# A fused attention and MLP kernel: tiles moved to multiples of 64 bytes, token sums formed a step earlier, five low parts given to GpSimd

## The chip, the cores and the metric

The kernel runs on one core of a Trainium2 chip. The metric is the device time of one execution in microseconds (us). The time before is the median of three runs; the profile is of one further execution.

## The reference

Three layers follow one another on a batch of 4 sequences of 768 tokens, 384 channels:

```
state = f_t * state + k_t v_t^T ;  y_t = q_t state          (gated linear attention, 8 heads of 48, f = sigmoid(f_logit))
u  = x + (U, V mixed over the tokens)                        (rank 32, x = the attention's output)
x2 = u + relu(u @ w_ch1) @ w_ch2                             (384 -> 1536 -> 384)
h  = relu(x2 @ w_in) ; c = conv3(h, conv_w)                  (384 -> 1024, over the tokens)
out = (h * sigmoid(c)) @ w_out                               (1024 -> 384)
```

The weights arrive as 64-bit floats and are turned into 32-bit ones in the kernel.

## The kernel before, in words

**Split products.** A 32-bit operand is held as a high part, rounded to the type F32R that TensorE reads, and a low part, the remainder. One product is then three matmuls: high by high, high by low, low by high. `split(src, hi, lo, eng)` makes the parts: ScalarE copies `src` into `hi` (L113), and the engine `eng` subtracts, `lo = src - hi` (L87).

**Stages.** From 0 to about 157 us the attention and the token mixing run, chunk by chunk. From 157 to 250 us the first MLP runs on the first 1024 tokens (t = 0): for each of its 12 blocks `u` and two halves `i`, `up1` makes 9 matmuls of 512 columns into a PSUM bank `a`, `relu` writes the high part with ScalarE (L287) and the low part with VectorE (L288), and `down1` makes 9 matmuls into the banks `b`. `relu` writes the pair `rh`, `rl`, but every third time one tile named `third` that holds both. During this stage the weights of the next blocks are still being made: three VectorE instructions `cvt` for a piece (L136 to L138), then ScalarE's cast into `w1h` or `w2h` (L113) and GpSimd's subtraction into `w1l` or `w2l` (L87). From 250 to 449 us the same MLP runs on the other two token blocks (t = 1, 2) in six groups each, in a Strassen-like form with sums of weights (`swh`, `swl`) and four sums of token blocks, so that a group has fewer products. From 449 us the second MLP runs with matmuls of 384 columns; they read tokens from `us` or `w2h`, and weights of 384 columns from `w1h`, `w1l`, as the moving operand.

**Two changes of token block.** A group of t reads its tokens from 18 slots of 512 columns: slots 0 to 11 are the tile `us`, slots 12 to 17 the tile `us2`. `value(kk, i, eng)` splits one token block into its slots; `total(n, eng)` makes the sum or difference number n on `eng`, and returns a function that splits it into its slots. Slots 12 and 13 hold the tokens (0, 0), 14 to 17 the sums 1 and 2. Before t = 1 (the first change, 217 to 251 us) these steps hang in the list `after` on steps (u, i) of t = 0. Before t = 2 (the second change, 335 to 355 us) they stand in `group`, and what can't be done in the last group of t = 1 goes into the list `carry`, which the first group of t = 2 empties.

**Order.** Each engine runs its instructions in the order in which the code records them. An instruction that waits holds all behind it on its engine.

**Where tiles lie.** The pools opened with `side="right"` are stacked down from the end of a partition. In the built program `u32` begins at byte 192,480, which is 32 beyond a multiple of 64, and so do `third`, `winh`, `winl`, `swh`, `swl`, `us2` and `spare`, and in the attention stage `uhl`, `vst`, `xh`, `xl`, `zst` and the tiles of queries, keys and values. The tiles `us`, `rh`, `rl`, `w1h`, `w1l`, `w2h`, `w2l` of the left side begin at multiples of 64.

Of the kernel before, what the change touches and what calls it, by code (L numbers as in the profile page):

```python
# [9 lines left out]
F32 = mybir.dt.float32  # L10
# [30 lines left out]
def kernel(  # L41
# [60 lines left out]
    w1l = const.tile([128, KD * DF1], F32R, name="w1l")  # L102
    w2h = const.tile([128, J1, DM], F32R, name="w2h")
    w2l = const.tile([128, J1, DM], F32R, name="w2l")
    u32_p = ctx.enter_context(tc.tile_pool(name="u32_p", bufs=1, side="right"))
    u32 = u32_p.tile([128, KD, B * S], F32, name="u32")
    w1hv = w1h.rearrange("p (a x) -> p a x", a=KD)
# [105 lines left out]
    def mlps(ms, banks, pieces, late, checks, hooks):  # L213
# [7 lines left out]
        u0 = us[:, 0:2 * KD * S].rearrange("p (i k s) -> p i k s", i=2, k=KD)  # L221
# [57 lines left out]
        def relu(ps, u, i):  # L279
            n = len(made)  # L280
            made.append((u, i))
            if win and n % 3 == 2:
                x = third([128, 2 * HT], F32R)
                rh, rl = x[:, 0:HT], x[:, HT:2 * HT]
            else:
                rh, rl = [rg.tile([128, HT], F32R, tag=x, name=x) for x in ("rh", "rl")]
            nc.scalar.activation(out=rh, in_=ps, func=ACTF.Relu)  # L287
            nc.vector.scalar_tensor_tensor(  # L288
                out=rl, in0=ps, scalar=0.0, in1=rh.bitcast(F32), op0=ALU.max, op1=ALU.subtract)
            downs.extend((rh, rl, u, i, m) for m in range(KD))  # L290
# [105 lines left out]
        def turnover(t):  # L396
            x = []
            ve, gp = nc.vector, nc.gpsimd

            def value(kk, i, eng):  # L400
                split(u_block(t, kk, i), *tokens_of(kk, i), eng)

            def total(n, eng):
                if t == 1:
                    dst = spare[0 if n == 3 else 1]
                else:
                    if not x:
                        x.append(ws_p.tile([128, 2 * 384], I32, tag="raw", name="sums", bufs=raw_bufs[0]).bitcast(F32)[:, 0:HT])
                    dst = x[0]
                b11, b12, b21, b22 = [u_block(t, *y) for y in ((0, 0), (0, 1), (1, 0), (1, 1))]  # L410
                a, b = {1: (b12, b11), 2: (b22, dst), 3: (b22, b12), 4: (b21, dst)}[n]
                sub(eng, dst, a, b)
                return lambda eng: split(dst, *token_sum(n), eng)

            return value, total

        n_group, carry = [0], []

        def group(t, p):
            j0, j1 = 2 * p, 2 * p + 1  # L420
            u0, u1 = t * J1 + j0, t * J1 + j1
# [5 lines left out]
            value, total = turnover(t + 1)  # L427
            ve, gp = nc.vector, nc.gpsimd
# [14 lines left out]
            nc.scalar.copy(out=s1, in_=pa)  # L443
            prod(pb, weight_sum(p, 1), token_sum(1), True)
            nc.scalar.copy(out=s5, in_=pb)
            for _ in range(min(2, len(carry))):
                carry.pop(0)()
            later(2)
            down1(2)
# [29 lines left out]
            prod(pw, weights(2, j0), tokens_of(2, 0))  # L479
            relu(pw, u0, 0)  # L480
            if not room:
                total(4, ve)(gp)
            later(room)
            down1(2)
# [1 line left out]
            relu(pz, u1, 1)  # L486
            if not room:
                carry.append(lambda: total(3, ve)(gp))
                carry.append(lambda: value(1, 1, gp))
                carry.extend(lambda a=a: value(*a) for a in ((2, 1, ve), (2, 0, gp), (1, 0, ve)))  # L490
            if ends_all:
                split_u(0)
            down1(1)
# [206 lines left out]
        u0, u1 = J1 - 2, J1 - 1  # L700
        items += [(up1, u0, 0), (up1, u0, 1), (down1, KD), (up1, u1, 0), (down1, KD), (up1, u1, 1), (down1, KD)]
        value, total = turnover(1)
        ve, gp = nc.vector, nc.gpsimd
        t_sums = {}

        def start_sum(n):
            t_sums[n] = total(n, ve)

        def end_sum(n):
            t_sums[n](ve)  # L710

        after = {}
        for p in range(J1 // 2 - 2):
# [2 lines left out]

            for x in range(4):
                after[2 * p + 2 + x // 2, x % 2] = [lambda k=x, f=lazy: f(k)]
        for at, f in (((8, 0), lambda: value(0, 0, ve)), ((9, 0), lambda: start_sum(1)), ((9, 0), lambda: end_sum(1)),
                      ((9, 1), lambda: start_sum(2)), ((9, 1), lambda: end_sum(2)), ((u0, 0), lambda: start_sum(4)),  # L720
                      ((u0, 1), lambda: start_sum(3)), ((u1, 0), lambda: end_sum(3)), ((u1, 0), lambda: value(1, 1, gp)),
                      ((u1, 0), lambda: end_sum(4)), ((u1, 1), lambda: value(1, 0, ve)), ((u1, 1), lambda: value(2, 0, gp)),
                      ((u1, 1), lambda: value(2, 1, ve))):
            after.setdefault(at, []).append(f)
# [32 lines left out]
        for i, (b, j) in enumerate(units):  # L757
# [6 lines left out]
            if i == len(units) - 1:  # L764
                last = gate_end(b, j)
# [23 lines left out]
    gc = gs.enter_context(tc.tile_pool(name="gc", bufs=1, side="right"))  # L789
    wk3 = gs.enter_context(tc.tile_pool(name="wk3", bufs=3, side="right"))  # L790
    wk2 = gs.enter_context(tc.tile_pool(name="wk2", bufs=2, side="right"))
    wk1 = gs.enter_context(tc.tile_pool(name="wk1", bufs=1, side="right"))
# [11 lines left out]
    dr = gs.enter_context(tc.tile_pool(name="gdr", bufs=1, space=bass.MemoryType.DRAM))  # L804
    ends_d = dr.tile([NG, 1, NP * 128], F32, name="ends_d")
    w_t = [gc.tile([MP, NP, D2], F32, name=f"w{i}") for i in range(2)]
    one = gc.tile([128, 1], F32, name="one")
    uhl = gc.tile([128, NCH, 2 * R], F32R, name="uhl")
    vst = gc.tile([3 * R, S], F32R, name="vst")
    a_t = [gc.tile([128, NP, 128], F32, name=f"a{i}") for i in range(3)]  # L810
# [339 lines left out]
    with tc.manual_schedule():  # L1150
# [200 lines left out]
        last = {}  # L1351

        def last_z():
            mix_in(NG - 1)
            last["z"] = mix_z(B - 1)
            last["g"] = g1 = wk1.tile([128, 1], F32, tag="g1", name="g1")
            nc.vector.tensor_reduce(out=g1[0:MP], in_=ga[0:MP].rearrange("p g a -> p (g a)"), axis=mybir.AxisListType.X, op=ALU.min)

        def last_add():
# [185 lines left out]
```

## Time and profile before

| | us |
|---|---|
| median of 3 runs | 653.61 (652.57 to 653.63) |
| profiled execution, whole | 656.3 |
| profiled execution, span of the trace | 654.6 |
| TensorE (PE) busy in the span | 634.9 |
| VectorE (DVE) busy | 456.9 |
| ScalarE (ACT) busy | 305.8 |
| GpSimd (POOL) busy | 192.5 |

The span runs from the first to the last recorded instruction; 1.7 us of the execution lie outside it. The end of a matmul is modelled and neighbours overlap, so that what a stretch of matmuls takes is read from start to start.

### The profile page before, as it was taken

The page shows a single profiled execution, that of the slowest core. Times are in us where ns is not written, and L with a number is a line of the kernel's source. Part 1 is how long each engine was busy: PE and PEld are TensorE (multiplying, and loading weights), DVE is VectorE, ACT ScalarE, POOL GpSimd, SP SyncE. Part 2 cuts the span into 40 slices and gives each one's busy share as a digit, 9 for nine tenths or more (in the row PEclk, how much of TensorE's full clock was granted, in tenths as well). Part 3 has the DMA queues.
Part 4 walks back from the last instruction along what each step waited for, and adds up shares of the span by engine and source line. Part 5 has one row for each costly group of instructions (what it writes and reads, how often), then busy time and mean ns, then how long its engine had stood idle before and what let it go on. Part 6 is the DMA issues. An engine that isn't in the chain of part 4 may idle for free.

```text
span 654.6 us, 12837 instructions
## 1 busy us (share of the span) xinstructions
PE 634.9 (97%) x5098; PEld 552.1 (84%) x5098; DVE 456.9 (70%) x715; ACT 305.8 (47%) x583; POOL 192.5 (29%) x247
## 2 busy tenths in 40 slices
PE   8999989999999989999998999999999999999995
PEld 6778868887887868888886888889999999999995
DVE  5867767786787887555556555668988777777762
ACT  6779757853223234333344333343544644634533
POOL 2167567662666638100033111112120110210000
PEclk9999989999999999999999999999999999999998
DMA  9787798730333310344400122121000200200202
GB/s 179 145 159 141 157 188 153 146 85 2 95 98 97 98 48 26 116 131 127 132 26 25 53 81 80 52 80 41 1 2 1 74 0 1 73 2 1 74 1 77
DMA packets 132953, 50.19 MB, mean 77 GB/s; under 512 B 113316, under 2 KB 128701, under 8 KB 132884
## 3 DMA queue, kind: packets, MB, share of 16 engines
q1 hardware_dynamic: 132884, 49.28, 30.8%
q8 instruction: 42, 0.69, 0.5%
q14 instruction: 27, 0.22, 0.1%
HBM read 44.50 MB, written 4.77 MB: 75 GB/s over the span
## 4 chain that ended last, share of the span: by engine, by line
PE 85%; DMA 4%; DVE 3%; POOL 2%; ACT 1%; issue 1%; SPq 1%; POOLq 0%; ACTq 0%; DVEq 0%
PE b L84 37%; PE a L84 36%; PE y L84 4%; DMA f<-in_f_logit_dram 4%; PE s L84 2%; PE n L84 1%; PE kTp L923 1%; PE qTp L923 1%; PE xt L1066 1%; PE z L84 1%; PE kv L84 1%; PE mix L84 1%; POOL sp L850 1%; POOL qh L889 1%; DVE us L87 1%
## 5 line engine op out<-in xcount | busy, mean ns | idle before, releaser
L84 PE MATMUL a<-us,w1h 128*128 128x512 f32 (+1 forms) x384 | 117.2, 386 | 3.6 <-DVE spare L439 2.4
L84 PEld LDWEIGHTS a<-us,w1h 128*128 128x128 f32 x384 | 71.4, 188 | 18.2 <-DVE spare L439 2.8
L84 PE MATMUL a<-us,w1l 128*128 128x512 f32 (+1 forms) x192 | 74.1, 386 | 0.7 <-POOL w1l L87 0.7
L287 ACT ACTIVATE rh<-a 128x512 fp32r<-128x512 f32 x49 | 29.2, 597 | 92.2 <-PE a L84 88.5
L288 DVE SCALAR_TENSOR_TENSOR rl<-a,rh 128x512 fp32r<-128x512 f32 x49 | 33.8, 690 | 48.8 <-ACT rh L287 48.8
L84 PE MATMUL b<-w1h,swl 128*128 128x384 f32 x192 | 64.5, 336 | 0.0
L84 PE MATMUL b<-w1h,swh 128*128 128x384 f32 x192 | 64.5, 336 | 0.0
L84 PE MATMUL b<-w1l,swh 128*128 128x384 f32 x192 | 64.5, 336 | 0.0
L84 PE MATMUL b<-rh,w2h 128*128 128x512 f32 x147 | 57.4, 390 | 0.0
L84 PE MATMUL b<-rh,w2l 128*128 128x512 f32 x147 | 57.4, 390 | 0.0
L84 PE MATMUL b<-rl,w2h 128*128 128x512 f32 x147 | 57.3, 390 | 0.0
L561 ACT ACTIVATE h<-a 128x384 f32<-128x384 f32 x64 | 30.9, 497 | 33.0 <-PE a L84 25.8
L991 DVE TENSOR_TENSOR p<-s,tri 128x512 f32<-128x512 f32 x48 | 30.9, 686 | 20.0 <-PE s L84 19.8
L84 PEld LDWEIGHTS a<-us,w1l 128*128 128x128 f32 x192 | 36.0, 188 | 9.5 <-POOL w1l L87 2.7
L84 PE MATMUL b<-third,w2h 128*128 128x512 f32 x138 | 43.3, 395 | 0.0
L84 PE MATMUL a<-us,winh 128*128 128x384 f32 x144 | 36.9, 338 | 0.0
L84 PE MATMUL a<-w2h,winh 128*128 128x384 f32 x144 | 36.7, 336 | 0.0
L84 PEld LDWEIGHTS b<-w1l,swh 128*128 128x128 f32 x192 | 36.1, 188 | 0.0
L84 PEld LDWEIGHTS b<-w1h,swl 128*128 128x128 f32 x192 | 36.1, 188 | 0.0
L84 PEld LDWEIGHTS b<-w1h,swh 128*128 128x128 f32 x192 | 36.1, 188 | 0.0
L87 POOL TENSOR_TENSOR w2h<-u,w2h 128x384 fp32r<-128x384 f32 x6 | 10.9, 1815 | 80.0 <-ACT w2h L113 80.0
L84 PEld LDWEIGHTS b<-rh,w2h 128*128 128x128 f32 x147 | 27.6, 188 | 6.1
(200 smaller groups left out, 1506.4 us busy)
## 6 DMA issues: line engine op xcount, KB each, us to landing
raw<-in_moe_w_ch_dram SPq DMA_DIRECT2D x48, 384.0 KB
k<-in_k_dram SPq DMA_DIRECT2D x24, 192.0 KB
q<-in_q_dram SPq DMA_DIRECT2D x24, 192.0 KB
v<-in_v_dram SPq DMA_DIRECT2D x48, 96.0 KB
f<-in_f_logit_dram SPq DMA_DIRECT2D x23, 192.0 KB
raw<-in_moe_w_in_dram SPq DMA_DIRECT2D x8, 384.0 KB
raw<-in_moe_w_out_dram SPq DMA_DIRECT2D x8, 384.0 KB
out_dram<-o SPq DMA_DIRECT2D x8, 192.0 KB
```

The source lines that it names most:

```text
L84: nc.tensor.matmul(out=out, lhsT=lhsT, rhs=rhs, start=start, stop=stop, skip_group_check=True)
L87: eng.tensor_tensor(out=out, in0=a, in1=b, op=ALU.subtract)
L287: nc.scalar.activation(out=rh, in_=ps, func=ACTF.Relu)
L288: nc.vector.scalar_tensor_tensor(out=rl, in0=ps, scalar=0.0, in1=rh.bitcast(F32), op0=ALU.max, op1=ALU.subtract)
L561: nc.scalar.activation(out=h[:, 1 + hf.start:1 + hf.stop], in_=ps, func=ACTF.Relu)
L850: nc.gpsimd.tensor_scalar(out=sp, in0=ft.pop(g), scalar1=LARGEST, scalar2=LEAST_LOGIT, op0=ALU.min, op1=ALU.max)
L889: (nc.gpsimd if g == 1 else eng).tensor_tensor(out=heads(q_t[g % 2]), in0=qt.pop(g), in1=heads(a_t[g % 3]), op=ALU.mult)
L923: nc.tensor.transpose(out=ps[:, p, :], in_=src[:, p, 0:MP], identity=ident)
L991: nc.vector.tensor_tensor(out=t, in0=sc[g][j], in1=tri.unsqueeze(1).to_broadcast([128, NP, C]), op=ALU.mult)
L1066: nc.tensor.transpose(out=ps[:, m * 128:(m + 1) * 128], in_=u32[:, m, g * C:(g + 1) * C], identity=ident)
```

## The change

A tile of 32 bytes, `edge`, is put at the very end of each partition, ahead of `u32`, and two one-column tiles take 64 bytes in place of 32. All the tiles named above then begin at multiples of 64 bytes (`u32` at 192,448); no instruction of the computation changes its shape by it. At the first change of token block the sums are formed a step ahead of their casts. At the second change `value(1, 1)` moves out of `carry` into the last group of t = 1, the first step of the next group takes one item of `carry` in place of two, and the low parts of (2, 1) and (1, 0) go from VectorE to GpSimd.

```diff
+    edge = ctx.enter_context(tc.tile_pool(name="edge", bufs=1, side="right"))
+    edge.tile([128, 8], F32, name="edge")
     u32_p = ctx.enter_context(tc.tile_pool(name="u32_p", bufs=1, side="right"))
...
-            for _ in range(min(2, len(carry))):
+            if carry:
                 carry.pop(0)()
...
             if not room:
+                value(1, 1, gp)
                 total(4, ve)(gp)
...
                 carry.append(lambda: total(3, ve)(gp))
-                carry.append(lambda: value(1, 1, gp))
-                carry.extend(lambda a=a: value(*a) for a in ((2, 1, ve), (2, 0, gp), (1, 0, ve)))
+                carry.extend(lambda a=a: value(*a, gp) for a in ((2, 1), (2, 0), (1, 0)))
...
-        for at, f in (((8, 0), lambda: value(0, 0, ve)), ((9, 0), lambda: start_sum(1)), ((9, 0), lambda: end_sum(1)),
-                      ((9, 1), lambda: start_sum(2)), ((9, 1), lambda: end_sum(2)), ((u0, 0), lambda: start_sum(4)),
+        for at, f in (((8, 0), lambda: value(0, 0, ve)), ((8, 1), lambda: start_sum(1)), ((9, 0), lambda: end_sum(1)),
+                      ((9, 1), lambda: start_sum(2)), ((u0, 0), lambda: end_sum(2)), ((u0, 1), lambda: start_sum(4)),
                       ((u0, 1), lambda: start_sum(3)), ((u1, 0), lambda: end_sum(3)), ((u1, 0), lambda: value(1, 1, gp)),
...
-    one = gc.tile([128, 1], F32, name="one")
+    one = gc.tile([128, 16], F32, name="one")[:, 0:1]
...
-            last["g"] = g1 = wk1.tile([128, 1], F32, tag="g1", name="g1")
+            last["g"] = g1 = wk1.tile([128, 16], F32, tag="g1", name="g1")[:, 0:1]
```

VectorE at the first change, from the ReLU's low part of (9, 0) to that of (10, 0), before. `spare<-u` is the subtraction that forms a sum, `us_3123<-spare` (the tile `us2`) its low part:

```order
L288 SCALAR_TENSOR_TENSOR rl<-a_3607,rh 128x512
L136 TENSOR_SCALAR cvt<-raw 128x384
L137 SCALAR_TENSOR_TENSOR cvt<-raw,cvt 128x384
L138 SCALAR_TENSOR_TENSOR cvt<-raw,cvt 128x384
L87 TENSOR_TENSOR spare<-u_76 128x512
L87 TENSOR_TENSOR us_3123<-spare,us_3123 128x512
L288 SCALAR_TENSOR_TENSOR rl<-a_3643,rh 128x512
L136 TENSOR_SCALAR cvt<-raw 128x384
L137 SCALAR_TENSOR_TENSOR cvt<-raw,cvt 128x384
L138 SCALAR_TENSOR_TENSOR cvt<-raw,cvt 128x384
L87 TENSOR_TENSOR spare<-u_76,spare 128x512
L87 TENSOR_TENSOR us_3123<-spare,us_3123 128x512
```

The same place of the changed program (lines are 2 higher there):

```order
L87 TENSOR_TENSOR spare<-u_80 128x512
L290 SCALAR_TENSOR_TENSOR rl<-a_3612,rh 128x512
L138 TENSOR_SCALAR cvt<-raw 128x384
L139 SCALAR_TENSOR_TENSOR cvt<-raw,cvt 128x384
L140 SCALAR_TENSOR_TENSOR cvt<-raw,cvt 128x384
L87 TENSOR_TENSOR us_3127<-spare,us_3127 128x512
L290 SCALAR_TENSOR_TENSOR rl<-a_3647,rh 128x512
L138 TENSOR_SCALAR cvt<-raw 128x384
L139 SCALAR_TENSOR_TENSOR cvt<-raw,cvt 128x384
L140 SCALAR_TENSOR_TENSOR cvt<-raw,cvt 128x384
L87 TENSOR_TENSOR spare<-u_80,spare 128x512
L290 SCALAR_TENSOR_TENSOR third<-a_3681,third 128x512
```

The first sum now stands ahead of the ReLU's low part of (9, 0), and its own low part after the next conversions; the second sum's low part has moved behind the conversions that follow `third`.

VectorE at the second change, in the first group of t = 2, before. `u_76<-b` is the last addition of `down1`, L439 the two additions of the Strassen form, `us<-u_76` the low parts of (2, 1) and (1, 0):

```order
L325 TENSOR_TENSOR u_76<-b_3922,u_76 128x512
L439 TENSOR_TENSOR a_4505<-a_4504,spare 128x512
L87 TENSOR_TENSOR us<-u_76,us 128x512 x2
L325 TENSOR_TENSOR u_76<-b_3926,u_76 128x512
L325 TENSOR_TENSOR u_76<-b_3880,u_76 128x512
L439 TENSOR_TENSOR spare<-a_4504,spare 128x512
L288 SCALAR_TENSOR_TENSOR rl<-a_4505,rh 128x512
```

The changed program at this place:

```order
L327 TENSOR_TENSOR u_80<-b_3926,u_80 128x512
L441 TENSOR_TENSOR a_4511<-a_4510,spare 128x512
L327 TENSOR_TENSOR u_80<-b_3930,u_80 128x512
L327 TENSOR_TENSOR u_80<-b_3884,u_80 128x512
L441 TENSOR_TENSOR spare<-a_4510,spare 128x512
L290 SCALAR_TENSOR_TENSOR rl<-a_4511,rh 128x512
```

The two low parts are gone from between the two additions.

GpSimd over the last group of t = 1 and the first of t = 2, before (`us_3123` is `us2`; `sums` holds a sum of token blocks):

```order
L87 TENSOR_TENSOR us_3123<-u_76,us_3123 128x512
L87 TENSOR_TENSOR us_3123<-sums,us_3123 128x512 x2
L87 TENSOR_TENSOR us<-sums,us 128x512 x2
L87 TENSOR_TENSOR us<-u_76,us 128x512 x2
L87 TENSOR_TENSOR w1l<-cvg,w1h 128x3x128 x8
```

The changed program:

```order
L87 TENSOR_TENSOR us_3127<-u_80,us_3127 128x512
L87 TENSOR_TENSOR us_3127<-sums,us_3127 128x512 x2
L87 TENSOR_TENSOR us<-u_80,us 128x512
L87 TENSOR_TENSOR us<-sums,us 128x512 x2
L87 TENSOR_TENSOR us<-u_80,us 128x512 x3
L87 TENSOR_TENSOR w1l<-cvg,w1h 128x3x128 x8
```

The low part of (1, 1) stands between the sums 2 and 4, and three low parts follow sum 3 where two did. The rows of PE and SP are the same in both programs but for lines and numbers.

## Rows read from the trace of the kernel before

**Rows 1.** Windows: stretch, its us, PE, PEld, DVE, ACT, POOL busy, clock, DMA.

```profile
157.00:226.00 69.00, 68.97 (x302) 55.89 (x301) 54.37 (x71) 17.44 (x34) 39.71 (x51) 1.00 0.29 87
226.00:242.00 16.00, 14.08 (x59) 10.32 (x58) 13.82 (x20) 5.07 (x10) 7.32 (x9) 1.00 0.23 74
344.00:355.00 11.00, 8.63 (x38) 6.68 (x36) 8.97 (x11) 4.83 (x9) 5.01 (x4) 1.00 0.11 36
449.00:655.00 206.00, 197.86 (x1138) 196.93 (x1136) 153.96 (x185) 97.49 (x172) 15.62 (x9) 0.99 0.07 24
```

**Rows 2.** Timeline, PE: start, us, instruction; a block of third, one of rh and rl.

```profile
213.30 0.63 PE L84 MATMUL b<-third,w2h 128*128 128x512 f32 x2
...
215.40 0.63 PE L84 MATMUL a<-us,w1h 128*128 128x512 f32 x2
...
217.49 0.39 PE L84 MATMUL b<-rh,w2h 128*128 128x512 f32 x1
...
219.53 0.62 PE L84 MATMUL a<-us,w1h 128*128 128x512 f32 x2
```

**Rows 3.** Groups of instructions by line, whole span: count, busy, mean ns.

```profile
L84 PE MATMUL b<-third,w2h 128*128 128x512 f32 x138 | 43.3, 395 | 0.0
```

**Rows 4.** Timeline, PE, products of tokens (0, 0) and sum 1 in a group of t = 1.

```profile
296.91 0.63 PE L84 MATMUL a<-us,w1h 128*128 128x512 f32 x2
...
298.31 0.40 PE L84 MATMUL b<-rh,w2h 128*128 128x512 f32 x1
```

**Rows 5.** Timeline, PE, two halts at the first change, in brackets idle time and releaser.

```profile
231.67 0.39 PE L84 MATMUL b<-rh,w2l 128*128 128x512 f32 x1
232.50 0.73 PE L84 MATMUL a<-us,w1h 128*128 128x512 f32 x2 [0.45 <-ACT w1h L113]
...
233.92 0.62 PE L84 MATMUL a<-us,w1h 128*128 128x512 f32 x2
...
239.15 0.39 PE L84 MATMUL b<-rh,w2l 128*128 128x512 f32 x1
240.32 0.73 PE L84 MATMUL a<-us,w1h 128*128 128x512 f32 x2 [0.78 <-ACT w1h L113]
...
241.74 0.63 PE L84 MATMUL a<-us,w1h 128*128 128x512 f32 x2
```

**Rows 6.** Timeline, DVE, the same place.

```profile
226.56 0.69 DVE L288 SCALAR_TENSOR_TENSOR rl<-a,rh 128x512 fp32r<-128x512 f32 x1 [0.96 <-ACT rh L287]
...
229.05 1.25 DVE L138 SCALAR_TENSOR_TENSOR cvt<-raw,cvt 128x384 int32<-128x384 int32 x1
...
231.59 0.69 DVE L87 TENSOR_TENSOR us<-spare,us 128x512 fp32r<-128x512 f32 x1 [0.69 <-ACT us L113]
...
239.17 0.56 DVE L138 SCALAR_TENSOR_TENSOR cvt<-raw,cvt 128x384 int32<-128x384 int32 x1
```

**Rows 7.** Timeline, ACT, the same place.

```profile
230.94 0.62 ACT L113 CAST us<-spare 128x512 fp32r<-128x512 f32 x1 [4.00 <-DVE spare L87]
...
231.95 0.50 ACT L113 CAST w1h<-cvt 128x384 fp32r<-128x384 f32 x1
```

**Rows 8.** Timeline, POOL, the same place.

```profile
240.35 1.00 POOL L87 TENSOR_TENSOR w1l<-cvt,w1h 128x384 fp32r<-128x384 f32 x1 [2.03 <-ACT w1h L113]
```

**Rows 9.** Timeline, POOL, DVE and PE at the second change.

```profile
348.57 3.00 POOL L87 TENSOR_TENSOR us<-u,us 128x512 fp32r<-128x512 f32 x2
...
348.83 3.29 DVE L87 TENSOR_TENSOR us<-u,us 128x512 fp32r<-128x512 f32 x2
...
350.06 0.62 PE L84 MATMUL a<-us,w1h 128*128 128x512 f32 x2
...
351.21 0.39 PE L84 MATMUL a<-us,w1l 128*128 128x512 f32 x1
...
353.24 0.67 DVE L439 TENSOR_TENSOR spare<-a,spare 128x512 f32<-128x512 f32 x1
...
353.97 0.73 PE L84 MATMUL a<-us,w1h 128*128 128x512 f32 x2 [2.37 <-DVE spare L439]
```

## The prediction

> **What bounds the kernel now.** I read the busy time by stretch first. From 157 us to the end TensorE is the pace: it is busy for 68.97 of 69.00 us up to 226, and for 197.86 of the last 206, where what is missing is the tail behind the last matmul [rows 1]. It halts in two places only, both at a change of token block: 226 to 242 us has 1.92 us without a matmul, 344 to 355 us has 2.37 [rows 1]. So time can come from two sources: the step from one matmul to the next, and these two halts. The attention stage ahead of 157 us is a mixture of waits on transfers, GpSimd, VectorE and TensorE; nothing in the change takes work off it.
>
> **Part 1, the addresses.** The reader should compare two blocks of nine matmuls with 512 columns that read the same weights. With `third` as moving operand, 32 bytes beyond a multiple of 64, the nine start at 213.30 and the next block at 215.40: 2.10 us, 233.3 ns each. With `rh` and `rl`, at multiples of 64, it is 217.49 to 219.53: 2.04 us, 226.7 ns each [rows 2]. The difference is 6.6 ns, some 16 of the 512 columns at 2.4 GHz, as if one more piece of 64 bytes were fetched; the reason doesn't matter for the sum.
>
> How many pay it: `third,w2h` has 138 records [rows 3], and the third matmul of each product reads `third` with `w2l`, so 207 in all, and 207 x 6.6 ns = 1.37 us. In the groups of t = 1 and 2 the product of tokens (0, 0) and that of sum 1 have their moving operand in `us2`. Those six take 296.91 to 298.31, 1.40 us, again 233.3 ns each [rows 4]. Sum 2 lies in `us2` too, and the product of sum 3 reads its weights from `swh`, `swl`: six more matmuls for which I have no block as clean; their excess is put between 0 and 6.6 ns, and I take the middle, 3.3. Per group that is 6 x 6.6 + 6 x 3.3 = 59 ns, in 12 groups 0.71 us. Part 1 gives 2.1 us.
>
> In the last stage nothing comes from it: all moving operands (`us`, `w2h`, `w1h`, `w1l`) lie at multiples of 64 already. In the attention stage the products of `xh`, `xl` and `vst` move too (about 72 matmuls, 0.5 us at 6.6 ns), but there others end the waits: I take 0 and keep 0.5 as a bound. So part 1 lies between 0 (if the 6.6 ns have another cause) and 2.6 us.
>
> The Trainium skill (SBUF — State Buffer, Specifications) speaks against this part: it gives SBUF cachelines of 16 bytes and a penalty for crossing into a new one. An offset of 32 is a whole number of such lines, so by that page the shift would change nothing. The trace doesn't agree, since the two blocks differ by 6.6 ns a matmul [rows 2]; what the page would make of the sum is rival B.
>
> **Part 2, the first change.** Two halts. From the start at 231.67 to that at 233.92 there are four matmuls, 0.91 us at 226.7 ns, but 2.25 us passed: 1.34 lost. From 239.15 to 241.74 it is 2.59, so 1.68 lost [rows 5]. (The idle times in brackets are shorter, since the restart itself is slow.)
>
> The first halt waits for `w1h`. Its conversion on VectorE ends at 229.05 + 1.25 = 230.30 [rows 6], but ScalarE casts it at 231.95 only. What stands between: ScalarE is held for 4.00 us by the cast of sum 1, which waits for VectorE's `spare`, and the ReLU and the cast of `w1h` stand behind it [rows 7]. In the changed order sum 1 is formed ahead of the ReLU's low part of (9, 0), where VectorE waited 0.96 us anyway [rows 6], so its 0.6 us is hidden there. (Without that cover it would delay the low part by 0.6 us, which a later block of `down1` reads.) ScalarE's cast of the sum then runs at once, the ReLU of (9, 1) when its product ends, and the cast of `w1h` at about 230.6. With 0.5 for it [rows 7] and 1.00 for GpSimd's `w1l` [rows 8] both are there by 232.1. TensorE wants `w1h` at 231.67 + 0.23 = 231.90 and `w1l` two matmuls later, at 232.35. The first halt goes: 1.34 us.
>
> The second halt waits for the next `w1h`, whose conversion ends at 239.17 + 0.56 = 239.73 [rows 6]. VectorE went from 230.30 to 239.73 without a pause but two: it formed two sums, each followed by a wait of 0.69 us for ScalarE's cast ([rows 6] show one; the other is its like) and a low part. The step of such a 0.69 us instruction to the next is about 0.6. The change takes out of this stretch sum 1 (0.6), both waits (1.4) and sum 2's low part (0.6), together 2.6. It puts in a wait for the ReLU of (10, 0), which VectorE now reaches too early, about 0.6. So the conversion ends 2.0 us earlier, at 237.7, the cast at 238.2, `w1l` at 239.3. TensorE comes 1.34 us earlier as well: it wants `w1h` at 239.38 - 1.34 = 238.04 and `w1l` at 238.5. A halt of about 0.8 us remains, and 0.8 of the 1.68 is won (bounds 0 and 1.68). What is late next is again `w1l`. Sums 4 and 3 stand together later, 1.2 us ahead of the ReLU's low part of (11, 0). Before they stood one step apart, and VectorE is idle there soon after; I put it at 0. Part 2 gives 1.34 + 0.8 = 2.1 us, bounds 1.3 and 3.0.
>
> **Part 3, the second change.** TensorE starts its last matmul before the halt at 351.21 and the next at 353.97 [rows 9]: 2.76 us for 0.23, 2.5 lost. It waits for VectorE's addition `spare` (L439), which frees its bank. Ahead of it on VectorE stand the two low parts, 3.29 us, and two additions of 353.24 - (348.83 + 3.29) = 1.1 us [rows 9]. Without the low parts the additions are done about 350.0. The addition `spare` itself needs the product before 350.06, whose last results land about 0.2 us later. It runs from about 350.3 to 350.95, and TensorE comes at 351.44. The halt goes: 2.5 us.
>
> The cover is GpSimd. It starts its low parts behind sum 3 at 348.57 and took 1.5 us for each [rows 9]. At that price (2, 1) is ready at 350.1, (2, 0) at 351.6, (1, 0) at 353.1. By the code's order TensorE takes (1, 1) at 350.06, (2, 1) three matmuls later, its low part one after that: 350.98, then (2, 0)'s at about 352.4 and (1, 0) behind nine more matmuls, near 354.9. Each is in time, by 0.8 us or more. (1, 1) itself moved ahead of sum 4: one more cast on ScalarE (0.6) and one more low part on GpSimd (1.5), while the slots of (1, 1) have been read. Sum 3 has to wait until GpSimd has read sum 4, so up to 1.5 us could be passed on to it. In the bounds I let part 3 fall to 1.0. The shorter first pop of `carry` changes only which step records what; the low parts are behind sum 3 either way. DMAs aren't moved.
>
> **Sum.** 2.1 + 2.1 + 2.5 = 6.7 us. The profiled execution, 656.3 us, would be 649.6. It is 2.7 above the median of the runs, and that is in no row that the change touches, so I take the 6.7 off the median: 653.6 - 6.7 = **646.9 us**.
>
> **Rivals.**
> - B: the 6.6 ns are not of the address (both halves of `third` are in one tile, `rh` and `rl` in two), or come from a source that stays. For: the nine matmuls from 215.40 to 217.49, between the two blocks compared, read `us` at multiples of 64 and took 2.09 us all the same [rows 2]; something else makes some blocks slow as well. Against: `us2` has no such pair and pays the same [rows 4]. Without part 1: 649.0. By the skill's page named above this is the case to expect.
> - C: VectorE remains the pace at the first change. Per half step it has a ReLU part, three conversions and one or two sums, some 4.4 us against 4.1 of TensorE's 18 matmuls. Then the first halt's gain is met again at the second and 3 is all that goes: 653.6 - 2.1 - 2.5 = 649.0.
> - D: GpSimd's queue takes the place of VectorE at the second change. It decides from 350.98 - 348.57 = 2.4 us for a low part on; the row has 1.5. Then most of part 3 is lost: 649.4.
> - E, the other side: with every tile at the same offset, reads of TensorE fall together with writes of ScalarE and VectorE that lay apart before, and each product pays. There are some 1,280 matmuls from 157 to 449 us (292 us at about 0.228) and 1,138 recorded behind that [rows 1]; against 4.6 us from parts 2 and 3 it costs time from 2.5 ns a product ((4.6 + 1.3) / 2,420). At 6.6 ns it is 16 us: 653.6 - 4.6 + 16 = 665. Against: `rh` and `rl` are written and read at multiples of 64 and are the fast ones [rows 2].
>
> **Chances.** My forecast, all three parts within their bounds: 0.60, with 645 to 648.5 as its own range. B 0.15, C 0.10, D 0.08, E 0.03, and 0.04 that several gains fail and under 1.3 us is left. A measurement of this kernel tells about 0.2% (1.3 us) from no change; the three runs span 1.1. Faster by more: 0.93, within: 0.04, slower: 0.03. The range takes the low bounds (part 1 at 2.6, part 2 at 3.0, part 3 at 2.5: 645.5, and half a microsecond of spread) and, above, cases B to D with the same spread: 645.0 to 650.0.
>
> **What would show it.** Right: `third` blocks at 2.04 us; in 226 to 242 us one halt in place of two, of about 0.8 us; none in 344 to 355; ScalarE's `us<-spare` with no wait for VectorE. Wrong: `third` still at 2.10 (B); a halt at `w1h` ended by VectorE of over 1.5 us (C); a halt behind 350 us ended by GpSimd's `us` (D); matmuls of the last stage further apart than now (E). A longer attention stage would upset the sum without touching any of its terms.

## The result, and the profile after

| | before | after |
|---|---|---|
| median of 4 runs each, us | 653.62 (652.57 to 654.92) | 646.67 (644.27 to 647.38) |
| ratio | | 0.9886 [0.9854, 0.9919] |
| profiled execution, whole | 656.3 | 646.12 |
| span of the trace | 654.6 | 644.4 |

The changed kernel is 6.95 us faster by the medians. The two profiled executions differ by 10.2 us, more than the medians do; where the other 3 us lie is told below.

Windows of the changed kernel by stretches of [rows 1] (the place of the old halt, 353.97 us before, is now at 346.03, so the stretch ahead of it is added). Columns: stretch, its us, busy time of PE, PEld, DVE, ACT, POOL with the number of instructions, granted clock, DMA share, GB/s.

```profile
226.00:242.00 16.00, 15.54 (x67) 12.13 (x66) 14.95 (x22) 6.20 (x12) 7.55 (x8) 1.00 0.17 49
...
250.00:344.00 94.00, 93.44 (x413) 77.06 (x412) 51.02 (x88) 34.80 (x62) 20.83 (x26) 1.00 0.31 97
344.00:355.00 11.00, 11.00 (x50) 9.13 (x49) 6.08 (x11) 3.51 (x6) 3.06 (x3) 1.00 0.11 36
```

At the first change TensorE is without a matmul for 0.46 us where it was 1.92 [rows 1]; in 344 to 355 us nothing is missing where 2.37 were. In their place stands a gap of 0.56 us in 250 to 344. The same stretch of the kernel before has none:

```profile
250.00:344.00 94.00, 94.00 (x410) 76.78 (x410) 50.38 (x88) 32.20 (x57) 21.31 (x30) 1.00 0.32 97
```

Timeline of TensorE in the changed kernel: start, us, instruction, in brackets idle time and releaser.

```profile
210.69 0.61 PE L84 MATMUL b<-third,w2h 128*128 128x512 f32 x2
...
212.73 0.61 PE L84 MATMUL a<-us,w1h 128*128 128x512 f32 x2
...
214.82 0.39 PE L84 MATMUL b<-rh,w2h 128*128 128x512 f32 x1
...
235.08 0.39 PE L84 MATMUL b<-rh,w2l 128*128 128x512 f32 x1
235.59 0.73 PE L84 MATMUL a<-us,w1h 128*128 128x512 f32 x2
236.67 0.50 PE L84 MATMUL a<-us,w1l 128*128 128x512 f32 x1 [0.35 <-POOL w1l L87]
237.01 0.63 PE L84 MATMUL a<-us,w1h 128*128 128x512 f32 x2
...
296.88 0.62 PE L84 MATMUL a<-us,w1h 128*128 128x512 f32 x2
...
298.24 0.62 PE L84 MATMUL a<-us,w1h 128*128 128x512 f32 x2
...
338.82 0.39 PE L84 MATMUL a<-us,w1l 128*128 128x512 f32 x1
339.76 0.72 PE L84 MATMUL a<-us,swh 128*128 128x512 f32 x2 [0.56 <-DVE third L290]
340.33 0.40 PE L84 MATMUL a<-us,swl 128*128 128x512 f32 x1
```

Three things are to be seen. The nine matmuls with `third` go from 210.69 to 212.73, 2.04 us where [rows 2] had 2.10, and six with the tokens (0, 0) and sum 1 from 296.88 to 298.24, 1.36 where [rows 4] had 1.40: all at 226.7 ns. The `us` block behind `third` still takes 2.09. The two halts of [rows 5] have become one: from 235.08 to 237.01 there are four matmuls, 0.91 us at 226.7 ns, but 1.93 us passed, so 1.0 is lost, and the last to come is GpSimd's `w1l`. And there is a new halt at 339.76: from 338.82 to 340.33 there are three matmuls, 0.68 us, and 1.51 passed: 0.83 lost.

What the engines beside it do there, timelines of VectorE, ScalarE and GpSimd in the changed kernel:

```profile
222.86 0.95 DVE L87 TENSOR_TENSOR spare<-u 128x512 f32<-128x512 f32 x1
...
227.58 0.68 DVE L87 TENSOR_TENSOR us<-spare,us 128x512 fp32r<-128x512 f32 x1
...
234.43 0.56 DVE L140 SCALAR_TENSOR_TENSOR cvt<-raw,cvt 128x384 int32<-128x384 int32 x1
...
336.07 1.76 DVE L87 TENSOR_TENSOR sums<-u,sums 128x512 f32<-128x512 f32 x1 [0.19 <-POOL us L87]
339.01 0.69 DVE L290 SCALAR_TENSOR_TENSOR third<-a,third 128x512 fp32r<-128x512 f32 x1 [1.18 <-ACT third L289]
```

```profile
224.18 0.62 ACT L115 CAST us<-spare 128x512 fp32r<-128x512 f32 x1
...
235.02 0.51 ACT L115 CAST w1h<-cvt 128x384 fp32r<-128x384 f32 x1 [0.89 <-DVE cvt L140]
...
337.87 0.62 ACT L115 CAST us<-sums 128x512 fp32r<-128x512 f32 x1 [2.20 <-DVE sums L87]
338.39 0.59 ACT L289 ACTIVATE third<-a 128x512 fp32r<-128x512 f32 x1
```

```profile
235.61 1.01 POOL L87 TENSOR_TENSOR w1l<-cvt,w1h 128x384 fp32r<-128x384 f32 x1 [2.03 <-ACT w1h L115]
...
336.00 1.29 POOL L87 TENSOR_TENSOR us<-u,us 128x512 fp32r<-128x512 f32 x1
...
343.26 3.79 POOL L87 TENSOR_TENSOR us<-u,us 128x512 fp32r<-128x512 f32 x3
```

At the first change, sum 1 is formed at 222.86 and cast at 224.18 without a wait; the 4.00 us for which it held ScalarE [rows 7] are gone, and so is VectorE's 0.69 ahead of the low part [rows 6]. What is left is a chain for the second `w1h`: conversion until 234.43 + 0.56 = 234.99, cast at 235.02, `w1l` from 235.61 to 236.62, matmul at 236.67.

At the second change read the chain backwards from 339.76: TensorE waits for VectorE's low part of `third` (339.01), that for ScalarE's ReLU (338.39), that stands on ScalarE behind the cast of sum 4 (337.87), and the cast waited 2.20 us for the sum, which took 1.76 us on VectorE. Beside it GpSimd runs the low part that the change moved here, `value(1, 1)`, from 336.00 to 337.29. Alone the same subtraction takes 0.69 us (as in the experiment `e4_early_value`, below). The sum ends at 337.83, 0.54 after GpSimd, so it seems hardly to have moved while GpSimd ran. The order itself makes the two meet: sum 4 is written over sum 2, so VectorE has to wait for GpSimd's low part of sum 2 (the 0.19 us in its row), and as that ends GpSimd goes on with (1, 1). ScalarE's extra cast isn't what is late, since ScalarE is idle for 2.20 us behind it. The slow sum agrees with the Trainium skill (SBUF — State Buffer, section SBUF: two separate sides), which says that a VectorE instruction with two inputs from SBUF and a GpSimd instruction that reads SBUF hold one pair of ports in turn, each for the whole instruction.

Of the low parts, those of (2, 1) and (1, 0) are the two that are new to GpSimd; the title's five is not what the program shows.

**The sum.** To leave the attention stage aside I measure from one fixed matmul (the 1,500th of the program, near 148 us before and 146 after) to the start of the last: 498.45 us before, 491.56 after, 6.9 less. That is as much as the medians differ. It consists of the first change, halts of 3.02 and now 1.0 (2.0 us); of the second, 2.64 with the slow restart and now 0.83 (1.8); and of 3.0 for shorter steps, counted as what the steps between consecutive recorded matmuls take over 226.7 ns (512 columns) in the first MLP: 0.96 + 2.59 us before (t = 0; t = 1 and 2), 0.52 + 0.01 after.

**The other 3 us of the profiled executions.** Of these 2.3 lie ahead of the fixed matmul and 1.0 behind the start of the last one. Windows of the kernel before, and then of the changed one, in the attention stage:

```profile
93.00:97.00 4.00, 3.62 (x53) 2.68 (x55) 2.87 (x5) 3.15 (x8) 3.81 (x6) 0.62 1.09 211
94.00:97.00 3.00, 2.72 (x43) 2.15 (x47) 2.22 (x5) 2.96 (x8) 2.81 (x5) 0.50 1.07 205
```

```profile
93.00:97.00 4.00, 3.85 (x99) 3.46 (x101) 3.34 (x7) 3.96 (x10) 3.73 (x6) 1.00 0.90 195
```

In the profiled execution of before TensorE stood at a granted clock of 0.50, which is 1.2 GHz, from 94 to 97 us, and recorded 53 matmuls in 93 to 97 us where the changed kernel has 99. This doesn't follow the change: `e1_addresses` (below), with the change's addresses, has 0.57 over 93 to 97 us, and `e2_first_change` and `e3_second_change`, without them, have 1.00. It fits that the profiled execution of before lay 2.7 us over its median. What the 1.0 us behind the last matmul is, the runs don't tell.

### The profile page after: what moved, and what is told of

Read it like the earlier page. It is cut to its first block, busy times and chain, and to the rows that moved or that the text cites. A ratio compares the mean times of both kernels' runs of the same rounds, so it can differ in the third digit from the quotient of the medians.

```text
span 644.4 us, 12837 instructions
## 1 busy us (share of the span) xinstructions
PE 630.6 (98%) x5098; PEld 551.7 (86%) x5098; DVE 455.5 (71%) x713; ACT 305.8 (47%) x583; POOL 195.4 (30%) x249
## 5 line engine op out<-in xcount | busy, mean ns | idle before, releaser
L87 POOL TENSOR_TENSOR us<-u,us 128x512 fp32r<-128x512 f32 (+1 forms) x16 | 21.7, 1368 | 41.3 <-ACT us L115 41.2
```

What stands on the lines that cost most here:

```text
L87: eng.tensor_tensor(out=out, in0=a, in1=b, op=ALU.subtract)
```

## The experiments

The first three make one part of the change alone in the kernel before, the fourth moves one step in the changed kernel; they ran with the kernel before on one chip (median 654.73 of 24 runs). The others ask what in the addresses counts; the kernel before took 654.05 us beside those with names in `e5` to `e8` and 655.71 beside those in `f` (medians of 7).

### The addresses alone

```diff
+    edge = ctx.enter_context(tc.tile_pool(name="edge", bufs=1, side="right"))
+    edge.tile([128, 8], F32, name="edge")
...
-    one = gc.tile([128, 1], F32, name="one")
+    one = gc.tile([128, 16], F32, name="one")[:, 0:1]
```

and the same for `g1`.

> The kernel before with the address part alone (edge and the two 64-byte tiles), both orders as before. Theory: the step of 226.7 ns holds everywhere behind 250 us, and the time from the first matmul of the first MLP to the last falls by the 3.2 us that the steps above 226.7 ns sum to in the trace before (3.5 us there, 0.3 in the changed kernel): about 650.5. Rival (the address does nothing of its own, the steps shortened because the halts went): the blocks of third stay at 2.10 us, 653.6.

Measured: 652.46 us, ratio 0.9964 [0.9941, 0.9987]. The steps alone give all of part 1: outside the two changes the stretches are as in the changed kernel, 3.0 us shorter than before. The two halts of the first change stay (1.5 and 1.7 us), and so does the one at 350 us. But the profiled execution shows a price behind that halt. Windows and timeline of this kernel:

```profile
350.00:356.00 6.00, 4.42 (x13) 3.50 (x14) 3.48 (x7) 1.78 (x3) 0.00 (x0) 0.75 0.00 0
```

```profile
348.69 0.39 PE L84 MATMUL a<-us,w1l 128*128 128x512 f32 x1
351.58 0.74 PE L84 MATMUL a<-us,w1h 128*128 128x512 f32 x2 [2.50 <-DVE spare L441]
...
354.04 0.63 PE L84 MATMUL b<-third,w2l 128*128 128x512 f32 x1
...
355.32 0.63 PE L84 MATMUL b<-third,w2l 128*128 128x512 f32 x1
```

Behind a wait of 2.50 us the granted clock fell (0.75 over these 6 us), and three matmuls from 354.04 to 355.32 take 1.28 us, 427 ns each in place of 227. Over the 60 matmuls about this change it cost 1.5 us (18.03 against 16.50). So this run shows part 1 at 3.0 less 1.5 (496.92 us from the fixed matmul to the last, 1.5 less than before), and a halt can cost more than its own length. The other runs fit: of the 12, the five with a mean granted clock of 0.996 or more took 649.31 to 650.66 us, near the 650.5 expected, and the seven with 0.993 to 0.995 took 652.38 to 655.58.

### The order at the first change alone

```diff
-        ... ((8, 0), lambda: value(0, 0, ve)), ((9, 0), lambda: start_sum(1)), ((9, 0), lambda: end_sum(1)),
-            ((9, 1), lambda: start_sum(2)), ((9, 1), lambda: end_sum(2)), ((u0, 0), lambda: start_sum(4)),
+        ... ((8, 0), lambda: value(0, 0, ve)), ((8, 1), lambda: start_sum(1)), ((9, 0), lambda: end_sum(1)),
+            ((9, 1), lambda: start_sum(2)), ((u0, 0), lambda: end_sum(2)), ((u0, 1), lambda: start_sum(4)),
```

> The kernel before with the first change of token block alone. Theory: from the start of the matmuls of (9, 0) to those of (11, 0) 2.0 us fall away, one halt of about 1.0 us is left there; blocks of third stay at 2.10 us and the halt of 2.5 us near 351 us stays: about 651.6. Rival (VectorE is the pace, the gain comes only together with the shorter steps): both halts keep 2.5 us or more, 653.6.

Measured: 653.22 us, ratio 0.9972 [0.9959, 0.9985]. Windows and timeline of TensorE in this kernel:

```profile
226.00:242.00 16.00, 15.54 (x67) 12.05 (x66) 14.92 (x22) 5.77 (x12) 7.40 (x10) 1.00 0.20 62
...
350.00:356.00 6.00, 5.60 (x17) 4.45 (x18) 2.94 (x5) 1.78 (x3) 0.00 (x0) 0.72 0.00 0
```

```profile
236.29 0.39 PE L84 MATMUL b<-rh,w2l 128*128 128x512 f32 x1
...
237.87 0.50 PE L84 MATMUL a<-us,w1l 128*128 128x512 f32 x1 [0.35 <-POOL w1l L87]
238.21 0.63 PE L84 MATMUL a<-us,w1h 128*128 128x512 f32 x2
```

The same one halt remains (236.29 to 238.21: 1.92 for four matmuls, 1.0 lost), so part 2 gives its 2.0 us without the others. The 60 matmuls about this change take 14.76 us in place of 16.75. Here too the clock fell behind the halt at 350 us (0.72), which hides 1.5 us of it in this profile.

### The order at the second change alone

```diff
-            for _ in range(min(2, len(carry))):
+            if carry:
                 carry.pop(0)()
...
+                value(1, 1, gp)
                 total(4, ve)(gp)
...
-                carry.append(lambda: value(1, 1, gp))
-                carry.extend(lambda a=a: value(*a) for a in ((2, 1, ve), (2, 0, gp), (1, 0, ve)))
+                carry.extend(lambda a=a: value(*a, gp) for a in ((2, 1), (2, 0), (1, 0)))
```

> The kernel before with the second change alone. Theory: the halt of 2.6 us near 351 us goes, and a new one of about 0.8 us stands some 12 us earlier, where VectorE's subtraction for sum 4 takes 1.8 us instead of 0.7 beside GpSimd's low part of (1, 1): net 1.8, about 651.8. Rival (the halt of 0.8 us comes from the shorter steps, not from the order): no new halt, 651.1.

Measured: 652.17 us, ratio 0.9968 [0.9953, 0.9983]. One row tells what it gives: the matmuls with `swl`, 36 of them, of which the first and the last are the same two products in every kernel here. From the first start to the last it is the groups of t = 1 and 2 with the second change between. The view is the tile `swl` on TensorE: count, duration in ns (least, median, most), first and last start. The kernel before, and this one:

```profile
L84 PE MATMUL a<-us,swl x36: 389/393/401, 250.5 to 431.7; 128*128 128x512 f32 x36
```

```profile
L84 PE MATMUL a<-us,swl x36: 389/393/401, 247.7 to 426.9; 128*128 128x512 f32 x36
```

181.2 us before, 179.2 here: 2.0 us, where 1.8 was expected. The new halt is there with the old, longer steps as well, 1.36 us for three matmuls, 0.68 lost. Timeline of TensorE in this kernel:

```profile
342.14 0.40 PE L84 MATMUL a<-us,w1l 128*128 128x512 f32 x1
342.94 0.73 PE L84 MATMUL a<-us,swh 128*128 128x512 f32 x2 [0.41 <-DVE third L288]
343.50 0.39 PE L84 MATMUL a<-us,swl 128*128 128x512 f32 x1
```

So the order makes it, not the faster steps.

### The low part of (1, 1) a step earlier

In the changed kernel, `value(1, 1, gp)` goes from ahead of `total(4)` to right behind the ReLU before it, where GpSimd's low part ends before VectorE wants to form sum 4.

```diff
             relu(pb, u0, 1)
+            if not room:
+                value(1, 1, gp)
             prod(pa, weights(1, j1), token_sum(4))
...
             if not room:
-                value(1, 1, gp)
                 total(4, ve)(gp)
```

> The changed kernel with value(1, 1) not ahead of sum 4 but two products earlier, behind the ReLU of its first bank. Theory: GpSimd is then done with (1, 1) before VectorE forms sum 2, sum 4 takes 0.7 us again, and the halt of 0.8 us at the second change goes: about 645.9. Rival (ScalarE's extra cast, not GpSimd's low part, is what held the ReLU of third): the cast is as long at its new place and a halt of 0.5 us or more stays, 646.7.

Measured: 646.05 us (642.82 to 646.66), ratio 0.9852 [0.983, 0.9874] to the kernel before. Timelines of VectorE and TensorE, and the row of `swl`, of this kernel:

```profile
336.67 0.69 DVE L87 TENSOR_TENSOR sums<-u,sums 128x512 f32<-128x512 f32 x1 [0.18 <-POOL us L87]
```

```profile
339.42 0.39 PE L84 MATMUL a<-us,w1l 128*128 128x512 f32 x1
339.64 0.62 PE L84 MATMUL a<-us,swh 128*128 128x512 f32 x2
```

```profile
L84 PE MATMUL a<-us,swl x36: 389/389/389, 246.3 to 422.4; 128*128 128x512 f32 x36
```

Sum 4 takes 0.69 us again, the halt is gone, and the stretch is 176.1 us; in the changed kernel it is 176.9 (below). Taking the overlap away takes the halt away, which shows its mechanism. This kernel has the lowest median of the study, but only the trace shows the 0.8 us: the medians (646.05, and 646.67 for the changed kernel, taken at another time) can't tell the two apart.

### Everything at 32 beyond a multiple of 64

Is it the multiple of 64? Without `edge` the right side begins at 32 mod 64 again, and 32 bytes ahead of `w1h` move the left side there too.

```diff
+    const.tile([128, 8], F32, name="pad")
     w1h = const.tile([128, KD * DF1], F32R, name="w1h")
...
-    edge = ctx.enter_context(tc.tile_pool(name="edge", bufs=1, side="right"))
-    edge.tile([128, 8], F32, name="edge")
```

> The changed kernel without the edge and with 32 bytes put ahead of w1h on the left side: every tile that the products of 384 and 512 columns read begins 32 beyond a multiple of 64, moving operands and weights alike. Theory A (a moving operand that begins 32 beyond needs one more piece of 64 bytes): all products of 512 columns step at about 233 ns, 1,250 x 6.6 ns = 8 us slower than the changed kernel, and those of 384 columns behind 449 us also step 5 ns or more later (1,150 x 5 = 6 us): 655 to 661. Theory B (what costs is that moving operand and weights lie differently): all steps at 226.7 and 173.3 ns, 646.7, though nothing lies at a multiple of 64.

Measured: 649.67 us, ratio 0.9935 [0.9913, 0.9957]. The row of `swl` in the changed kernel, then in this one:

```profile
L84 PE MATMUL a<-us,swl x36: 389/389/397, 245.7 to 422.6; 128*128 128x512 f32 x36
```

```profile
L84 PE MATMUL a<-us,swl x36: 389/389/398, 248.3 to 425.2; 128*128 128x512 f32 x36
```

176.9 us in both. With no operand at a multiple of 64 every step is as short as in the changed kernel, and from the fixed matmul to the last it is 491.40 us (491.56 there). So a multiple of 64 isn't what counts in these stages; what the two kernels have in common is that both sides begin at the same place. The total missed both forecasts, 649.67 where theory B had 646.7: the attention stage took 2.5 us longer in this profile, with more waits of TensorE for ScalarE and GpSimd, and all four runs (649.00 to 650.15) are slower than the changed kernel's. Its tiles moved too; whether their place costs something there, these runs don't tell.

### Third, or the weights, out of step

Three kernels move one group of tiles in the changed one. To make room, three small tiles were joined, and that moved the whole left side by 64 bytes as well, which wasn't meant; the places that came about are in the table below.

```diff
-                x = third([128, 2 * HT], F32R)
+                x = third([128, 2 * HT + 16], F32R)[:, 8:2 * HT + 8]
```

(`e7_third_at_16` has 4 in place of 8, for 16 bytes.)

```diff
             mw = ms.enter_context(tc.tile_pool(name="mw", bufs=1, side="right"))
+            mw.tile([128, 8], F32, name="pad0")
             win.extend(mw.tile([128, KD, 128 * W_IN], F32R, name=n) for n in ("winh", "winl"))
             sw.extend(mw.tile([128, (J1 // 2) * 3 * 128], F32R, name=n) for n in ("swh", "swl"))
+            mw.tile([128, 8], F32, name="pad1")
```

> The changed kernel with third alone begun 32 beyond a multiple of 64. Both theories: blocks of nine with third at 2.10 us, 207 x 6.6 ns = 1.4 us. Open: whether neighbouring blocks with other operands get slower too, as those at 2.07 to 2.09 us in the trace before; if so 1.4 to 2.4 us between the first and the last product of 512 columns, if not 1.4.

> The changed kernel with third alone begun 16 beyond a multiple of 64. If any offset from 64 brings one more piece (theory A), or operands that lie differently (theory B): 2.10 us a block as at 32. If the loss grows with the bytes beyond 64 it is less, about 2.07; if pieces of 16 or 32 bytes are what counts, 2.04 at 16 only in the first case.

> The changed kernel with winh, winl, swh and swl alone begun 32 beyond a multiple of 64; they are only ever weights. Theory A (only the moving operand counts): all steps as in the changed kernel. Theory B (operands that lie differently): the products of the three sums, 108 matmuls of 512 columns, step at 232 ns or more, about 0.6 us over both token blocks, and the stage behind 449 us stays at 173.3 ns as it did before.

Measured, one run each: 651.95, 652.72 and 647.9 us. The steps with `third` as moving operand take 233 ns at 32 bytes and 231.8 at 16; those with `swh`, `swl` as weights 32 bytes off take 231.9 in the third kernel. So either operand counts. By the Trainium skill's cacheline of 16 bytes alone (SBUF — State Buffer, Specifications) all three would be without effect, 16 and 32 being whole lines; the runs don't agree, with 5 to 7 ns a matmul. But in the first two also the last stage, where `third` isn't read, was slower, and the shift of 64 is the only other thing that differs there. That led to the next four.

### The left side moved by 64, 128 and 256 bytes

In the changed kernel a row buffer of 512 bytes moves into the last stage's tiles, and the room goes into a pad ahead of `w1h`. All tiles stay at multiples of 64.

```diff
-    low_row = const.tile([1, 128], F32, name="low_row")
+    rows = {}
...
+    const.tile([128, 16], F32, name="pad")
     w1h = const.tile([128, KD * DF1], F32R, name="w1h")
```

(32 and 64 columns for 128 and 256 bytes. A fourth has no pad, but `third` 32 bytes on, as above, in a tile that is 512 bytes longer, so that nothing else moves.)

> The changed kernel with the tiles of the left side (us, rh, rl, w1h, w1l, w2h, w2l and the weight pieces) moved by 64 bytes, net of 512 bytes taken out below them by moving one row buffer of the last stage. Every tile still begins at a multiple of 64, but the two sides now lie 64 apart within 128 or 512 bytes. Theory (what costs is that moving operand and weights begin at different places within 128 bytes or more): products that read one operand of each side, those of third, us2, swh and swl with 512 columns, step at 232 ns or more, and those behind 449 us that read winh or swh at about 176 instead of 173.3: 2.7 us for that stage, some 2.6 for the Strassen-like groups, 652. Rival (multiples of 64 suffice, as the change has it): 646.7.

> The same with 128 in place of 64. If the place within 128 bytes is what counts, all steps are those of the changed kernel, 226.7 and 173.3 ns. If it is the place within 256 or 512 bytes, the steps are as with 64, about 5 us more.

> The same with 256. If the place within 128 or 256 bytes is what counts, the steps are those of the changed kernel. If it is the place within 512 bytes, the steps are as with 64.

> The changed kernel with third alone begun 32 bytes later, all else where it was (the earlier run of that name had moved the left side by 64 too). Blocks of third step at 233 ns: 207 matmuls, 1.3 us. Blocks behind or ahead of them with other operands: if they get slower too, as the sum over the trace before suggests (0.9 us there in matmuls whose own operands agree), the loss is 1.8 to 2.3 us in all; if not, 1.3.

Measured: 648.9 us, ratio 0.9906 [0.9877, 0.9936], for 64 bytes; one run each for the others, 651.75, 646.6 and 650.89. The row of `swl` with the left side moved by 64, 128 and 256, and with `third` moved by 32:

```profile
L84 PE MATMUL a<-us,swl x36: 390/393/394, 245.7 to 424.9; 128*128 128x512 f32 x36
```

```profile
L84 PE MATMUL a<-us,swl x36: 387/396/398, 246.6 to 425.6; 128*128 128x512 f32 x36
```

```profile
L84 PE MATMUL a<-us,swl x36: 389/389/389, 246.1 to 423.0; 128*128 128x512 f32 x36
```

```profile
L84 PE MATMUL a<-us,swl x36: 389/389/397, 248.2 to 426.7; 128*128 128x512 f32 x36
```

179.2, 179.0, 176.9 and 178.5 us. A shift of 64 or 128 bytes gives back all that the addresses gained in this stretch (the kernel with the order of the second change alone has 179.2), though every tile still lies at a multiple of 64; a shift of 256 costs nothing. For the last stage the chain of waits in time order shows blocks of 18 matmuls of 384 columns (start, us, engine and line). The changed kernel, then the shifts by 64 and by 128:

```profile
565.87 3.12 PE a L84 x18
```

```profile
564.96 3.12 PE b L84 x18
568.08 3.14 PE a L84 x18
```

```profile
484.87 3.17 PE b L84 x18
```

So there 64 bytes cost little and 128 cost 0.05 us a block, some 2.5 us over the stage; for 64 a cost there like that of the `e6` kernel (175.9 ns a step against 173.4) was expected and didn't come.

All kernels together; places are the first byte modulo 256 in the built programs, "stretch" is that from the fixed matmul to the last one:

| kernel | left (`us`, `rh`, `w1h`, `w2h`) | `third` | `swh`, `swl` | `us2` | `swl` row, us | last stage, ns a step | stretch, us |
|---|---|---|---|---|---|---|---|
| before | 192 | 224 | 224 | 224 | 181.2 | 173.6 | 498.45 |
| changed | 192 | 192 | 192 | 192 | 176.9 | 173.4 | 491.56 |
| e5, all at 32 | 224 | 224 | 224 | 224 | 176.9 | 173.4 | 491.40 |
| f5, left by 256 | 192 | 192 | 192 | 192 | 176.9 | 173.4 | 491.22 |
| f3, third by 32 | 192 | 224 | 192 | 192 | 178.5 | 173.4 | 493.64 |
| e8, weights | 128 | 128 | 160 | 192 | 178.4 | 173.5 | 493.03 |
| f1, left by 64 | 0 | 192 | 192 | 192 | 179.2 | 173.5 | 494.31 |
| f2, left by 128 | 64 | 192 | 192 | 192 | 179.0 | 175.7 | 496.48 |
| e6, third by 32 | 128 | 160 | 192 | 192 | 179.2 | 175.9 | 497.17 |
| e7, third by 16 | 128 | 144 | 192 | 192 | 179.3 | 176.2 | 497.42 |

Only the kernels in which all places agree are at 176.9. With different places the step of 512 columns goes from 226.7 to between 230 and 236 ns, by kernel and product, and matmuls near such ones pay too: with `third` alone moved by 32, the 691 steps of t = 1 and 2 whose operands agree average 227.8 ns, 0.75 us in all, beside the 1.06 us of the 152 with `third`. Those that pay stand behind a block of `third`: the first six behind it average 231.1 ns, from the eighth on it is 226.8, and the one directly ahead has 227.0.

## Why the prediction was right, and where its terms were off

The forecast was 646.9 us, the median is 646.67; its three parts were 2.1, 2.1 and 2.5, the stretches show 3.0, 2.0 and 1.8. The sum came out by luck: two errors offset one another.

**Part 1, the addresses: mis-sized, 2.1 predicted, 3.0 measured, and with a wrong reason.** The price of 6.6 ns for a matmul with operands apart was right (`third` went from 233.3 to 226.7). What the term left out is the neighbours: in the kernel before, the 619 steps of t = 1 and 2 whose operands agree averaged 228.6 ns, and they fell to 226.8 as well, 1.1 us beside the 1.8 of the 278 steps whose operands lie apart. [Rows 4] had the sign of it, and the prediction read it as something else: the product of sum 1 isn't apart, since `us2` and its weights `swh`, `swl` both lie 32 beyond a multiple of 64 (table above), and its three matmuls were slow (230.3 ns, against 234.3 for those of the tokens (0, 0)) as neighbours. So of the 12 matmuls a group that it counted besides `third`, six, those of sums 1 and 2, pay nothing of their own. In the last stage, which it took at 0 since the moving operands lie at multiples of 64, the weights `winh` and `swh` lay 32 off; there that cost little, 173.6 ns a step before and 173.4 after, 0.2 us. The "one more piece of 64 bytes" is refuted: nothing lies at a multiple of 64 in the kernel with all at 32, and it is as fast; everything does in that with the left side moved by 64, and its groups of t = 1 and 2 are as slow as before. By the table, the `edge` helps since it brings the right side to the same place modulo 256 as the left. That the reason "doesn't matter for the sum" held for this change alone; as a rule for the next kernel it would have misled.

**Part 2, the first change: right.** The halt of 1.34 us went; of the second 1.0 is left where 0.8 was predicted, and `w1l` is what is late, as said. ScalarE's cast without a wait and VectorE's new wait for the ReLU (0.6 predicted, 0.52 in the trace at `third`) came as worked out. What would shorten the remaining chain wasn't tried.

**Part 3, the second change: mis-sized, 2.5 predicted, 1.8 net.** The halt of 2.5 us (2.64 with the slow restart) went as predicted and GpSimd was in time for all that it took over. The step that failed is "(1, 1) itself moved ahead of sum 4: one more cast on ScalarE (0.6) and one more low part on GpSimd (1.5)". It counted who waits in GpSimd's queue (sum 3, up to 1.5 us) and not who runs beside it: VectorE's sum 4 took 1.76 us in place of 0.69, ScalarE's ReLU stood behind its cast, and TensorE lost 0.83 us at 339.76, 27 matmuls (6.3 us) ahead of the place of the old halt. [Rows 9] had the sign of it: two low parts in 3.29 us on VectorE, where one alone takes 0.69 [rows 6], and two in 3.00 on GpSimd at the same time, where GpSimd now needs 3.79 for three, 1.26 each (343.26 above).

**The rivals.** B (the addresses have no effect) fell with the first experiment. Its argument, the `us` block of 2.09 us without an offset operand, is not answered by it: that block still takes 2.09 (212.73 to 214.82 above), so it has another cause, which stays open. The answer that the prediction gave B, that `us2` "pays the same", holds for the tokens (0, 0) and not for sum 1. C (VectorE remains the pace) and D (GpSimd's queue) fell with the halts: what is left at the first change is 1.0 us, and a low part takes 1.26 against the 2.4 at which D decides. E (all tiles at one offset collide) is the opposite of what these kernels show: of the places tried, the same one is the best.

**Open.** Why, of the differences tried (16, 32, 64, 128 and 256 bytes), only 256 is free, why the next few matmuls pay, and why the last stage hardly minds the left side 64 bytes further on than the right (f1, 173.5 ns) but does mind it 64 bytes less (e6, 175.9). Nor is it shown that a matmul's own two operands are the pair that counts. While a matmul runs, the weights of the next are loaded (in the changed kernel's 250 to 344 us PEld is busy for 77.06 us beside PE's 93.44), and in `e8_weights_at_32` 24 matmuls whose own operands agree, but whose successor's weights `swh` lie 32 off from them, take 235 ns each, while 11 whose successor has only its moving operand elsewhere take 226 or 227. So the moving operand of one matmul and the weights of the next may be the pair; no kernel here was built to tell. About 0.5 us of long steps remains in t = 0 in every kernel here, the 2.09 us block among them.

## What to carry to other kernels

Compare blocks of equal matmuls start to start: a few ns in each are a source of time on an engine that never waits, and in this kernel's MLP stages it was enough to bring the tiles of both operands to the same place modulo 256 bytes, wherever that is. When work moves to GpSimd, look not only at its queue but at which VectorE instructions with two inputs from SBUF will run beside it, and put it where VectorE pauses. A gain found in one stage is best measured between two fixed instructions of that stage, since waits elsewhere change from one execution to the next.

## What was not expected of the hardware

- A different place of moving operand and weights costs 4 to 9 ns of 227 at 512 columns, and the matmuls near it 1 to 2 on average; the absolute place (32 bytes tried) costs these matmuls nothing that could be seen.
- A subtraction of two tiles on VectorE took 1.76 us beside a GpSimd subtraction and 0.69 without.
- Behind halts of 2.5 us near 350 us the granted clock fell to 1.2 GHz in two kernels (`e1_addresses`, `e2_first_change`; 0.75 and 0.72 over 350 to 356 us), at 1.5 us each, and behind the same halt in the kernel before it didn't (1.00 over 344 to 355 us [rows 1]); in the attention stage it did at 94 us in some executions. In the profiles of the kernels without this halt it stayed at 1.00 there.
